# Pooled and banded attention with a gated feed-forward layer on one core: a written step order for the fill and the first eight slots, and seven products for half of the first w_out block

## The chip, the cores and the metric

The kernel runs on one core of one Trainium2 chip. The metric is the device time of one execution in microseconds (us), lower is better. Before the change the median of 5 runs was 346.57 us (345.24 to 352.35).

The core's engines work side by side, each through its own list of instructions in order: PE (matrix products, with PEld loading weights), DVE (vector), ACT (activations), POOL (general), and SP, which here only issues transfers. They meet at semaphores. PE writes its products to eight banks (`ps`), from which DVE and ACT read them.

## The reference

For 8 batches and 8 heads of 576 positions and 64 columns, the attention is the sum of two parts: one over sequences pooled four to one, repeated back, and one over a band of positions less than 4 apart. Its output, seen as 4608 tokens by 512, goes through a gated layer with 1536 inner columns.

```python
q_d = q.reshape(B, H, Sd, 4, D).mean(axis=3)      # k_d, v_d likewise
out_up = np.repeat(sm_attn(q_d, k_d, v_d), 4, axis=2)
mask = np.abs(pos[:, None] - pos[None, :]) < 4
out_local = softmax(np.where(mask, scale * q @ k.T, -1e9)) @ v
x = (out_up + out_local).transpose(0, 2, 1, 3).reshape(4608, 512)
out = (np.maximum(x @ w_gate, 0) * (x @ w_val)) @ w_out
```

## The kernel before

**Units of work.** Heads are taken two at a time: 32 pairs, four to a batch. Tokens of the gated layer are taken in 9 chunks of 512. The attention runs ahead of the layer, by four pairs at first (`LEAD`), because a chunk needs `xT`, the attention's output, of four pairs. So the program has a fill (pairs 0 to 3, with no layer yet), slots 0 to 7 (one pair each, chunks 0 and 1 beside them), steady periods (`emit_periods`, four pairs and one chunk each) and a tail. Each period follows the written order `ORDER`, the tail follows `TAIL`: tokens name a step, and each engine gets the steps' instructions in that order. Fill and slots were written as nested function calls (`emit_fill`, `emit_slot`, `LEAD_IN`).

**A pair.** q, k and v are loaded by POOL's transfers as 16-bit values (`qk`, `vw`; q of pair 0 by SP as 32-bit values, then cast on ACT). For pairs 0 to 8, PE flips q and k in 24 small products of 120 columns (L328): 96 columns are the transposed block, 24 the pooled sums. DVE and ACT copy them out (L348, L350). From pair 9 on a transposing transfer of SP does it (L302) and DVE pools (L309). Then come the scores, pooled (L389) and banded (L400); their exponentials on ACT (L410, L424); the mask on DVE (L416); the pooled v, which pairs 0 to 8 get from PE (L373) with a copy on ACT (L380), and the others from POOL in two additions (L355, L361) of v loaded a second time (L297). The output is made in one of three ways:
- pairs 0 to 3: output products with positions as rows (L447 pooled, L456 banded), reciprocals and multiplications on DVE (L464 to L474) into `xo`, which PE turns back to `xT` (L601, L605) and DVE or ACT copies (L614 to L617);
- pairs 4 to 8: softmax sums (L486, L495) and outputs (L505, L514) as separate half-array products, the sums' logarithm and exponential on ACT (L523, L525), one multiplication on DVE (L528) and one addition into `xT` (L538);
- from pair 9: outputs and sums in one whole-array product (L552, L560), with ACT and DVE working on 64 partitions at a time (L570, L575, L579).

**A chunk.** For each of 12 blocks of inner columns, four products with w_gate and four with w_val (L622), 128 by 512 each; relu on ACT (L639) and the product of the two on DVE (L643) into `gT`. The products with w_out: chunk 0 by 4 blocks of 12 products of 512 columns (L652), one in each of slots 4 to 7, copied out by ACT and stored by ACT's queue. From chunk 1 on, a `Unit` for each half chunk does it with seven products of 6 steps of 256 columns (L718), as in Strassen's scheme, for which DVE forms sums of `gT` (L712) and joins results (L755 to L767), ACT keeps partial results (L752), and DVE once forms four differences of w_out (L685, `emit_wt`).

**Fillers.** Products of zeros (`emit_warm`, L825) stand in the fill, where PE would have nothing to do: ten at the start, 19 of 512 columns afterwards.

**Loads in the fill.** POOL issues q, k and v of pairs 0 to 3, the first slice (of four) of w_gate and w_val, pairs 4 and 5, slice 1, pair 6, slice 2, pair 7, slice 3, q, k and v of pair 8, and four slices of w_out (L262, L292, L794, L800). A slice serves three of the twelve blocks.

Of the kernel before, what the change touches and what calls it, by code (L numbers as in the profile page):

```python
# [17 lines left out]
LEAD_IN = """  # L18
hg/3 relu/3 o/b00 o/b01 o/b10 o/b11 ln/b0 ln/b1 hv/3 gate/3 inv/b hg/4 relu/4 hv/4 xn/b0 gate/4
hg/5 relu/5 hv/5 xn/b1 xsum/b  # L20
# [35 lines left out]
LATE = ("gate/5/1", "next/0/1", "next/1/1")  # L56
# [61 lines left out]
def kernel(  # L118
# [26 lines left out]
    NVP = 9  # L145
# [10 lines left out]
    ffn = ctx.enter_context(tc.tile_pool(name="ffn", bufs=3))  # L156
# [38 lines left out]
    q32 = q32full[0:96]  # L195
    gT = ring(2, [128, NJJ, TCH], FP16, "gT_")
# [3 lines left out]
    wt4 = [xT[:, 0:3, 0:TCH].rearrange("p k (h d) -> p k h d", h=2)]  # L200
    wt4 += [t.rearrange("p (k h) d -> p k h d", h=2) for t in wtnew]
# [42 lines left out]
    def emit_load_qk(hp):  # L244
        for i in range(4):
            emit_load_q1(hp, i)

    def emit_load_q1(hp, i):

        b, off = head_off(hp)  # L250
        src, dst, hh = (q, k)[i // 2], qk16[hp % NL][:, i // 2, :], i % 2
        if hp < NTP:
            if hh:
                return
            if hp == 0 and src is q:
                nc.sync.dma_start(
                    q32.rearrange("p (n d) -> p n d", d=64),
                    _dap(src, off, [[D, 96], [NQ * D, 2 * NB], [1, D]]),
                )
                nc.scalar.copy(out=dst, in_=q32)  # L260
            else:
                nc.gpsimd.dma_start(  # L262
                    dst.rearrange("p (n d) -> p n d", d=64),
                    _dap(src, off, [[D, 96], [NQ * D, 2 * NB], [1, D]]),
                )
            return
        nc.gpsimd.dma_start(  # L267
            dst.rearrange("p (j h d) -> p j h d", h=2, d=64)[:, :, hh, :],
            _dap(src, off + hh * S * D, [[D, 96], [NQ * D, NB], [1, D]]),
        )  # L270
# [45 lines left out]
    def emit_qkT_pe(hp, b0, b1, b0_last=False):  # L316
        r, r4, r2 = hp % NL, hp % 4, hp % 2
        sv = qk16[r].rearrange("p i (h j d) -> p i h j d", h=2, d=64)
        blocks = list(range(2 * NB))
        if hp == 0:  # L320
            blocks = blocks[NB:] + blocks[:NB]
        elif b0_last:
            blocks = blocks[4:] + blocks[:4]
        for n in blocks:
            lo = 120 * (n % 4)
            bank = b0 if n < 4 else b1 + n // 4 - 1
# [8 lines left out]
        big = qkT[r4][:, 0 : 2 * S].rearrange("p (b n t) -> p b n t", b=3, n=4)  # L335
        sml = qkd[r2].rearrange("p i t -> p (i t)").rearrange("p (b n t) -> p b n t", b=3, n=4)
        act, dve = nc.scalar.copy, nc.vector.tensor_copy
        if hp == 0:
            plan = ((2, 1, act), (2, 0, act), (1, 1, dve), (1, 0, dve), (0, 1, act), (0, 0, dve))
        elif b0_last:  # L340
            plan = ((1, 1, act), (1, 0, act), (2, 1, dve), (2, 0, dve), (0, 1, dve), (0, 0, act))
        else:
            plan = ((0, 1, act), (0, 0, act), (1, 1, dve), (2, 1, dve), (2, 0, dve), (1, 0, act))
        for i, pooled, copy in plan:
            bank = b0 if i == 0 else b1 + i - 1
            t = ps[:, bank, 0:480].rearrange("p (n t) -> p n t", n=4)
            if pooled:
                copy(out=sml[:, i], in_=t[:, :, 96:120])  # L348
            else:
                copy(out=big[:, i], in_=t[:, :, 0:96])  # L350
# [16 lines left out]

    def emit_vd(hp, bank):
        t = vw[hp % NL][:, :, 0:64].rearrange("p (h j) d -> p j h d", h=2)
        o = ps[:, bank, 0:256].rearrange("p (c h d) -> p c h d", c=2, h=2)  # L370
        for c in range(2):
            for sig in range(3):
                nc.tensor.matmul(  # L373
                    out=o[:, c, :, :],
                    lhsT=pool_sb[0:WK, sig, :],
                    rhs=t[:, 3 * c + sig, :, :],
                    start=(sig == 0),
                    stop=(sig == 2),
                )
        nc.scalar.copy(  # L380
            out=vd[hp % 3].rearrange("p c (x d) -> p c x d", x=3)[:, :, 0:3:2, :], in_=o[0:72]
# [49 lines left out]
    def emit_s1(hp, p0):  # L431
        emit_s1_mm(hp, p0)
        for g in range(2):
            emit_exp(hp, p0, g)
            emit_mask(hp, g)
        emit_ed(hp, p0)

    def emit_s2(hp, bank, pu):
        r2 = hp % 2
        x = xo[hp % 3]  # L440
        vflat = vw[hp % NL].rearrange("p b c -> p (b c)")
        for hh in range(2):
            for tcx in range(2):
                for c in range(2):
# [4 lines left out]
                        lhsT=ed[r2][:, hh, s0 : s0 + 128],  # L449
# [3 lines left out]
                    )  # L453
        for hh in range(2):
            for j in range(NB):
                nc.tensor.matmul(  # L456
                    out=ps[:, 2 * pu + hh, 65 * j : 65 * j + 65],
                    lhsT=ee[r2][:, hh, NQ * j : NQ * j + 128],
# [4 lines left out]
        rd = small.tile([72, 2, 2], FP32, name="rd", tag="rd")  # L463
        nc.vector.reciprocal(out=rd, in_=_sap(ps, (0, 72), 512 * bank + 64, [[66, 2], [65, 2]]))  # L464
        nc.vector.tensor_tensor(
            out=x[0:72, NB : NB + 2, :].rearrange("p t (h d) -> p h t d", h=2),
            in0=_sap(ps, (0, 72), 512 * bank, [[131, 2], [65, 2], [1, 64]]),
            in1=_sap(rd, (0, 72), 0, [[2, 2], [1, 2], [0, 64]]),
            op=ALU.mult,
        )  # L470
        ru = small.tile([96, 2, NB], FP32, name="ru", tag="ru")
        nc.vector.reciprocal(out=ru, in_=_sap(ps, (0, 96), 1024 * pu + 64, [[448, 2], [65, NB]]))
        for j0, j1 in ((0, 3), (3, 6)) if hp == LEAD - 1 else ((0, 6),):
            nc.vector.tensor_tensor(  # L474
                out=x[:, j0:j1, :].rearrange("p j (h d) -> p h j d", h=2),
                in0=_sap(ps, (0, 96), 1024 * pu + 65 * j0, [[513, 2], [65, j1 - j0], [1, 64]]),
                in1=_sap(ru, (0, 96), j0, [[NB, 2], [1, j1 - j0], [0, 64]]),
                op=ALU.mult,
            )

    def emit_s2t_mm(hp, den, num):
        r2 = hp % 2
        e, d = ee[r2], ed[r2]
        for g in range(2):
            for hh in range(2):
                nc.tensor.matmul(  # L486
                    out=ps[64 * hh : 64 * hh + 64, den + g, 0:288],
                    lhsT=ones_sb[0:WK, 0:64],
                    rhs=e[:, hh, 288 * g : 288 * g + 288],
# [3 lines left out]
            for c in range(2):  # L493
                for hh in range(2):
                    nc.tensor.matmul(  # L495
                        out=ps[64 * hh : 64 * hh + 64, den + g, 288:360],
                        lhsT=ones_sb[0:72, 64:128],
                        rhs=d[:, hh, c * SD + 72 * g : c * SD + 72 * g + 72],
                        start=(c == 0),
                        stop=(c == 1),  # L500
                    )
        for g in range(2):
            for j in range(3):
                for hh in range(2):
                    nc.tensor.matmul(  # L505
                        out=ps[64 * hh : 64 * hh + 64, num + g, NQ * j : NQ * j + NQ],
                        lhsT=vw[hp % NL][:, NB * hh + 3 * g + j, 0:64],
                        rhs=e[:, hh, 288 * g + NQ * j : 288 * g + NQ * j + NQ],
                        start=True,
                        stop=True,  # L510
                    )
            for c in range(2):
                for hh in range(2):
                    nc.tensor.matmul(  # L514
                        out=ps[64 * hh : 64 * hh + 64, num + g, 288:360],
                        lhsT=vd[hp % 3][:, c, 128 * hh : 128 * hh + 64],
                        rhs=d[:, hh, c * SD + 72 * g : c * SD + 72 * g + 72],
                        start=(c == 0),
                        stop=(c == 1),
                    )  # L520

    def emit_rden(den, between=lambda: None):
        nc.scalar.activation(out=rden, in_=ps[:, den : den + 2, 0:360], func=AF.Ln)  # L523
        between()
        nc.scalar.activation(out=rden, in_=rden, func=AF.Exp, scale=-1.0)  # L525
# [3 lines left out]

    def emit_s2t(hp, between):  # L530
        emit_s2t_mm(hp, 4, 2)
        emit_rden(4, between)
        emit_xn(2)
        emit_xsum(hp)
# [51 lines left out]
    def emit_s2w(hp):  # L586
        for hh in range(2):
            for g in range(2):
                emit_s2w_mm(hp, hh, g)
        for hh in range(2):  # L590
            emit_ln(hh)
        emit_inv()
        for hh in range(2):
            emit_xnw(hh)

    def emit_x_pe(hp, pp):
        b, kk = hp // NPB, hp % NPB
        x = xo[hp % 3]
        for g in range(2):
            flat = pair(pp)[:, g, 0:288]  # L600
# [595 lines left out]
```

## Time and profile before

| | us |
|---|---|
| Median of 5 runs (range) | 346.57 (345.24 to 352.35) |
| The profiled execution | 345.24 |
| Its span, first instruction to last | 343.3 |
| PE busy in the span | 336.0 |
| DVE, ACT, POOL busy | 289.9, 215.3, 189.8 |
| First product of chunk 0 with weights (L622) starts | 24.82 |
| First w_out product of the steady periods (L718) starts | 95.07 |

The profile is of one execution. Times of places count from the start of the span. A line such as "17.11 0.60 PE L825 MATMUL ps<-zero_sb 128*128 128x512 f16 x2" gives start, busy time, engine, line of the kernel, operation, what it writes and reads, array rows by columns, and how many instructions were merged; brackets at its end give idle time of the engine before it and what ended it. A matrix product shown as busy overlaps the next, so PE's pace is read from start to start.

### The profile page before, as it was taken

The numbers are of one execution on the slowest core, as the hardware profiler recorded it, in microseconds if no ns is written. First come the engines' busy times: TensorE is split into PE (matmuls) and PEld (weight loads), VectorE is DVE, ScalarE is ACT, GpSimd is POOL, SyncE is SP. The second block draws the span as 40 slices with busy tenths as digits, with TensorE's granted clock in tenths as the row PEclk, the third lists the DMA queues.
The fourth block names the chain that finished last, engine by engine and source line by source line (L and its number), as shares of the span: only waits on it lengthen the run. The fifth ranks groups of instructions, "written<-read, shape, count | busy, mean of one in ns | idle before, by whom it ended". The sixth has DMA issues, their size and how long they took to land.

```text
span 343.3 us, 8159 instructions
## 1 busy us (share of the span) xinstructions
PE 336.0 (98%) x3187; PEld 210.4 (61%) x3187; DVE 289.9 (84%) x529; ACT 215.3 (63%) x410; POOL 189.8 (55%) x233
## 2 busy tenths in 40 slices
PE   6999999999999999999999999999999999999996
PEld 2665555555565756565666656665766557767785
DVE  5895667788899999999999999999999798886892
ACT  3767776677666776677667767776677633334222
POOL 8986656999999894988298879840300000000000
PEclk9999999999999999999999999999999999999999
DMA  9999999999999999999999997991100001001023
GB/s 152 166 170 186 187 189 169 165 152 184 186 155 174 163 170 93 136 157 148 114 113 158 153 126 82 174 133 37 51 13 32 32 0 48 31 33 60 30 65 110
DMA packets 168774, 40.31 MB, mean 117 GB/s; under 512 B 150080, under 2 KB 165664, under 8 KB 168736
## 3 DMA queue, kind: packets, MB, share of 16 engines
q0 software_dynamic: 132960, 22.93, 90.6%
q1 hardware_dynamic: 35056, 15.79, 23.4%
q10 hardware_dynamic: 720, 1.08, 1.0%
q8 instruction: 25, 0.41, 0.5%
q14 instruction: 13, 0.11, 0.1%
HBM read 46.45 MB, written 9.44 MB: 163 GB/s over the span
## 4 chain that ended last, share of the span: by engine, by line
PE 92%; DVE 3%; DMA 2%; ACT 1%; issue 1%; ACTq 0%; POOLq 0%
PE ps L622 50%; PE ps L718 20%; PE ps L928 4%; PE ps L552 3%; PE ps L652 3%; PE ps L400 2%; PE ps L389 2%; PE ps L328 2%; PE ps L560 2%; DMA qk<-in_k_dram 1%; DVE xo L474 1%; PE ps L486 1%; PE ps L373 0%; DMA out_dram<-y_sb 0%; PE ps L601 0%
## 5 line engine op out<-in xcount | busy, mean ns | idle before, releaser
L622 PE MATMUL ps<-xT,wv_sb 128*128 128x512 f16 x432 | 109.3, 379 | 0.0
L622 PE MATMUL ps<-xT,wg_sb 128*128 128x512 f16 x352 | 89.1, 380 | 0.1
L643 DVE TENSOR_TENSOR gT<-r,ps 128x512 f16<-128x512 f16 x88 | 59.2, 681 | 12.0 <-ACT r L639 6.3
L639 ACT ACTIVATE r<-ps 128x512 f16<-128x512 f32 x88 | 52.3, 595 | 26.6 <-PE ps L622 26.4
L622 PEld LDWEIGHTS <-wv_sb 128*128 128x128 f16 x432 | 41.0, 98 | 41.6
L622 PEld LDWEIGHTS <-wg_sb 128*128 128x128 f16 x352 | 32.0, 98 | 32.3 <-DVE xT L615 0.6
L579 DVE TENSOR_TENSOR xn<-ps,rden 64x720 f16<-64x720 f32 x46 | 41.7, 906 | 6.3 <-ACT rden L575 5.2
L410 ACT ACTIVATE ee<-ps 112x576 f16<-112x576 f32 x64 | 38.1, 648 | 10.4 <-PE ps L400 9.3
L570 ACT ACTIVATE rden<-ps 64x720 f32<-64x720 f32 x46 | 35.2, 765 | 14.7 <-PE ps L560 13.7
L267 POOL DMA_DIRECT2D qk<-in_q_dram x46 | 33.7, 735 | 5.1 <-DMA wo_sb<-in_moe_w_out_dram 2.8
L361 POOL TENSOR_TENSOR vd<-v 72x256 f16<-72x256 f32 x23 | 20.0, 877 | 29.8 <-PE ps L560 29.2
L416 DVE TENSOR_TENSOR ee<-ee,cst_sb 112x576 f16<-112x576 f16 x64 | 32.1, 521 | 3.2 <-ACT ee L410 2.2
L267 POOL DMA_DIRECT2D qk<-in_k_dram x46 | 33.7, 735 | 2.0 <-DMA qkT<-qk 1.2
L718 PEld LDWEIGHTS <-gT 128*128 128x128 f16 x288 | 28.2, 98 | 8.6
L292 POOL DMA_DIRECT2D vw<-in_v_dram x30 | 28.5, 949 | 7.7 <-PE ps L622 3.3
L309 DVE TENSOR_REDUCE qkd<-qkT 128x288 f16<-128x1152 f16 x23 | 30.9, 1344 | 0.4 <-DMA qkT<-qk 0.4
L355 POOL TENSOR_TENSOR v<-v 72x512 f32<-72x512 f16 x23 | 28.4, 1233 | 1.8 <-DMA v<-in_v_dram 1.2
L718 PEld LDWEIGHTS <-xo 128*128 128x128 f16 x240 | 22.8, 98 | 6.0 <-DVE xo L712 0.3
L752 ACT COPY q<-ps 128x256 f32<-128x256 f32 x39 | 14.5, 372 | 18.4 <-PE ps L718 17.6
L718 PE MATMUL ps<-wo_sb,gT 128*128 128x256 f16 x192 | 24.9, 273 | 0.0
L938 ACT COPY vw<-ps 128x256 f32<-128x256 f32 x30 | 10.8, 374 | 20.7 <-PE ps L928 13.8
L538 DVE TENSOR_TENSOR xT<-xn 128x576 f16<-128x576 f16 x28 | 21.9, 783 | 0.6
(115 smaller groups left out, 569.6 us busy)
## 6 DMA issues: line engine op xcount, KB each, us to landing
out_dram<-y_sb SPq DMA_DIRECT2D x20, 256.0 KB, 3.2
vw<-in_v_dram POOLq DMA_DIRECT2D x30, 168.0 KB, 6.6
qk<-in_q_dram POOLq DMA_DIRECT2D x46, 72.0 KB, 6.0
qk<-in_k_dram POOLq DMA_DIRECT2D x46, 72.0 KB, 5.8
v<-in_v_dram POOLq DMA_DIRECT2D x23, 144.0 KB, 6.4
out_dram<-y_sb SPq DMA_DIRECT2D x22, 128.0 KB, 1.7
wg_sb<-in_moe_w_gate_dram POOLq DMA_DIRECT2D x4, 384.0 KB, 9.6
wv_sb<-in_moe_w_val_dram POOLq DMA_DIRECT2D x4, 384.0 KB, 10.6
```

Of the source, the lines that this page charges most:

```text
L267: nc.gpsimd.dma_start(dst.rearrange("p (j h d) -> p j h d", h=2, d=64)[:, :, hh, :], _dap(src, off + hh * S * D, [[D, 96], [NQ * D, NB], [ ...
L292: nc.gpsimd.dma_start(t, _dap(v, base, [[D, WK], [NQ * D, n], [1, D]]))
L309: nc.vector.tensor_reduce(out=qkd[hp % 2].rearrange("p i t -> p (i t)"), in_=qkT[hp % 4][:, 0 : 2 * S].rearrange("p (t f) -> p t f", f=4), ...
L355: nc.gpsimd.tensor_tensor(out=m, in0=t[:, :, 0:128], in1=t[:, :, 128:256], op=ALU.add)
L410: nc.scalar.activation(out=o, in_=ps[0:WK, p0 + 2 * g : p0 + 2 * g + 2, 0:288], func=AF.Exp, scale=scale)
L416: nc.vector.tensor_tensor(out=o, in0=o, in1=_sap(masks_sb, (0, WK), 288 * g, [[0, 2], [1, 288]]), op=ALU.mult,)
L570: nc.scalar.activation(out=rden[lo : lo + 64], in_=ps[de : de + 64, 4 + 2 * hh : 6 + 2 * hh, 0:360], func=AF.Ln)
L579: nc.vector.tensor_tensor(out=xn[lo : lo + 64], in0=ps[lo : lo + 64, 4 + 2 * hh : 6 + 2 * hh, 0:360], in1=rden[lo : lo + 64], op=ALU.mult,)
L622: nc.tensor.matmul(out=pair(pp)[:, which, :] if out is None else out, lhsT=w[:, kk, bass.ts(jj, 128)], rhs=xT[:, kk, c * TCH : (c + 1) * TCH],
L639: nc.scalar.activation(out=r1, in_=pair(pp)[:, 0, :] if h1 is None else h1, func=AF.Relu)
L643: nc.vector.tensor_tensor(out=gT[c % 2][:, jj, :], in0=r1, in1=pair(pp)[:, 1, :] if h2 is None else h2, op=ALU.mult)
L718: nc.tensor.matmul(out=out, lhsT=left[:, i, :], rhs=right[i], start=(first and i == 0), stop=(i == NK - 1), skip_group_check=True,)
```

## The change

- Fill and slots 0 to 7 are no longer function calls but one written list, `FRONT`, whose tokens name a step, its pair or block and often the bank and the engine that copies. Every former function that issued several steps is split: a flip into three groups of eight products (`tr/pair/group/bank`) with copies placed by themselves (`ev`), sums and outputs of a pair into halves (`den`, `num`), output products into pooled and banded (`sd`, `su`), a turn back into halves (`xp`, `xe`), pooled v and its copy (`vd`, `vc`), a w_out block into quarters (`y`). Tokens with `@` are steps of the periods' kind.
- Chunk 0: half 0 (two blocks) keeps the plain w_out products, half 1 is done by a `Unit` (`p/..@1`, `sum`, `keep`, `c11` to `c22`). The plain results are stored by SP's queue, not ACT's.
- `NVP` goes from 9 to 11: pairs 9 and 10 get their pooled v from PE too, and their second load of v and POOL's additions go. Pair 8 changes from separate sums to the joint form.
- Fillers: 12 of 512 columns at the start, then 31 of 248 columns.
- v of pair 8 is loaded after w_out's slices and q and k of pair 9. The order of the loads ahead of that stays.
- The first layer products of chunk 0 stand before pair 3's output, and for single depth steps (`hv/0/0/7`: block 0, depth 0, bank 7).
- Relu results lie in a fixed ring of three, the places of w_out's differences are exchanged, and one more gate of chunk 1 is issued with the first steady period (`LATE`).

```diff
+FRONT = """
+pads loadk/0 loadv/0 loadq/1 loadk/1 loadv/1 loadq/2 cast loadk/2 tr/0/2/4 tr/0/1/3 ev/0/21V/4
+loadv/2 tr/0/0/2 ev/0/20V/4 ev/0/10A/3 vd/0/6 ev/0/01A/2 ev/0/00A/2 loadq/3 ev/0/11A/3 vc/0/6
+warm/6 tr/1/0/7 loadk/3 s1/0/2 ev/1/00A/7 tr/1/1/0 ev/1/01A/7 loadv/3 ed/0/2 tr/1/2/1 ev/1/20V/1
+ev/1/11A/0 warm/2 sd/0/6 ex/0/0/2 wg/0 ev/1/21V/1 rd/0/6 td/0/6 ev/1/10A/0 wv/0 ma/0/0 ex/0/1/2
+warm/7 s1/1/0 ones/4 vd/1/6 ma/0/1 ex/1/1/0 su/0/4 loadq/4 ed/1/0 ru/0/4 tu/0/1/4 ex/1/0/0
+warm/4 tr/2/1/2 loadk/4 tu/0/0/4 tr/2/2/3 ev/2/10A/2 tr/2/0/0 ev/2/21V/3 xp/0/1/5 ev/2/20V/3
+loadv/4 ev/2/11A/2 xp/0/0/4 ev/2/00A/0 ma/1/0 ev/2/01A/0 vc/1/6 ma/1/1 warm/3 s1/2/0 ones/5
+xe/0/0A/4 xe/0/1V/5 sd/1/6 ed/2/0 loadq/5 su/1/4 rd/1/6 td/1/6 ex/2/1/0 ru/1/4 warm/3 vd/2/6
+loadk/5 tu/1/1/4 ex/2/0/0 tr/3/1/2 tu/1/0/4 tr/3/2/3 loadv/5 vc/2/6 tr/3/0/0 ev/3/20V/3
+ev/3/10A/2 xp/1/0/4 xp/1/1/5 ma/2/1 ev/3/00A/0 sd/2/6 ev/3/21V/3 xe/1/1V/5 ev/3/11A/2 ev/3/01A/0
+wg/1 ma/2/0 xe/1/0A/4 warm/3 s1/3/0 rd/2/6 td/2/6 su/2/4 ed/3/0 vd/3/6 ru/2/4 tu/2/1/4 ex/3/0/0
+warm/3 hv/0/0/7 tu/2/0/4 wv/1 hv/0/1/7 ex/3/1/0 hv/1/0/1 ma/3/0 xp/2/1/5 vc/3/6 xp/2/0/4 ones/6
+ma/3/1 tr/4/0/0 xe/2/0A/4 xe/2/1V/5 sd/3/6 ev/4/00A/0 hv/1/1/1 loadq/6 rd/3/6 su/3/4 td/3/6
+ev/4/01A/0 hv/0/2/7 ru/3/4 hg/1/0/0 loadk/6 tu/3/1/4 tr/4/1/2 hv/1/2/1 ev/4/10A/2 tu/3/0/4
+tr/4/2/3 loadv/6 hg/0/0/6 ev/4/11A/2 ev/4/20V/3 xp/3/1/5 xp/3/0/4 ev/4/21V/3 hg/1/1/0 xe/3/1V/5
+wg/2 xe/3/0A/4 hg/1/2/0 hg/1/3/0 s1/4/2 wv/2 relu/1/0 hv/1/3/1 ex/4/0/2 hv/0/3/7 gate/1/1
...
+flip/9 num/7/1/7 tr/8/0/0 ev/8/21V/3 inv qk/a3/1@0 ev/8/20V/3 hv/11/*/1 ev/8/01V/0 ev/8/11V/2
+v/a/1@0 ev/8/00A/0 xn/6 y/1/0/3 y/1/1/3 qk/b0/1@0 gate/11/1 scores/a/0@1 xsum/7 qk/b1/1@0 vd/8/1
+exp/a0/0@1 y/0/0/2 qk/b2/1@0 vc/8/1 mask/a0/0@1 y/0/1/2 exp/a1/0@1 sum/0/1@1 qk/b3/1@0 hg/0/0@1
...
+sum/3/1@1 ln/b0/0@1 o/b11/0@1 vd/10/0 sum/2/1@1 p/1/1@1 ln/b1/0@1 pool/a/0@1 v2/b/0@1 hv/2/0@1
...
 """
-LATE = ("gate/5/1", "next/0/1", "next/1/1")
+LATE = ("gate/5/1", "gate/4/1", "next/0/1", "next/1/1")
-    NVP = 9
+    NVP = 11
-    def emit_qkT_pe(hp, b0, b1, b0_last=False):
...
+    def emit_flip(hp, i, bank):
+
+        sv = qk16[hp % NL].rearrange("p i (h j d) -> p i h j d", h=2, d=64)
+        for n in range(4 * i, 4 * i + 4):
             lo = 120 * (n % 4)
...
+    def emit_flipped(hp, i, pooled, eng, bank):
...
+        copy_on(eng)(out=o[:, i], in_=t[:, :, 96:120] if pooled else t[:, :, 0:96])
-    def emit_y(c, ty, bank, cut=0, inner=None):
...
+    def emit_y(c, ty, q, bank):
+        for jj in range(3 * q, 3 * q + 3):
             nc.tensor.matmul(
-                out=y_ps,
+                out=ps[:, bank, :],
                 lhsT=gT[c % 2][:, jj, bass.ts(ty, 128)],
                 rhs=wo_sb[:, jj, :],
                 start=(jj == 0),
                 stop=(jj == NJJ - 1),
             )
...
-        emit_out(c, ty, y_sb, nc.scalar)
+        emit_out(c, ty, y_sb, nc.sync)
...
+    def emit_front(tok):
+        kind, *a = tok.split("/")
+        if "@" in tok:
+            emit_step(kind, a[0], *map(int, a[1].split("@")))
         else:
+            FRONT_STEPS[kind](*[int(x) if x.isdigit() else x for x in a])
...
-        emit_warm(10)
-        emit_qkT_pe(0, 2, 3)
-        emit_pads()
-        emit_warm(3)
-        for hp in range(LEAD):
-            emit_fill(hp)
-        gate = None
-        for s in range(PS):
-            gate = emit_slot(s, gate)
+        emit_warm(12, True)
+        for tok in FRONT.split():
+            emit_front(tok)
         emit_periods(PS // 4, (NP - LEAD) // 4)
```

## The prediction

> **What bounds the kernel now.** The page first: which engine has no air, and whether the clock is granted.
>
> ```profile
> PE 336.0 (98%) x3187; PEld 210.4 (61%) x3187; DVE 289.9 (84%) x529; ACT 215.3 (63%) x410; POOL 189.8 (55%) x233
> ...
> PE   6999999999999999999999999999999999999996
> PEclk9999999999999999999999999999999999999999
> DMA  9999999999999999999999997991100001001023
> ...
> PE 92%; DVE 3%; DMA 2%; ACT 1%; issue 1%; ACTq 0%; POOLq 0%
> ```
>
> PE is busy from slice 2 to the end at full granted clock, and the chain that ended last is PE for 92%. But a filler product counts as busy too, so the question is what PE's first stretch holds. Next the same view by stretches: the fill, chunk 0, the rest of what the change rewrites, and one steady period.
>
> ```profile
> 6.31:24.82 18.51, 16.87 (x331) 12.22 (x331) 16.15 (x49) 12.08 (x30) 17.27 (x22) 1.00 2.20 166
> 24.82:57.60 32.78, 32.66 (x420) 18.18 (x416) 21.07 (x44) 24.86 (x50) 19.15 (x25) 1.00 1.73 185
> 57.60:95.07 37.47, 37.47 (x312) 18.95 (x307) 29.79 (x40) 25.98 (x42) 35.86 (x44) 1.00 1.88 170
> ...
> 130.86:166.00 35.14, 35.14 (x324) 21.93 (x323) 33.73 (x52) 24.92 (x45) 26.80 (x33) 1.00 1.65 140
> ```
>
> Columns: stretch, length, PE, PEld, DVE, ACT, POOL busy with counts, granted clock, DMA, GB/s. From 24.82 on PE is full; only the fill has idle time. The order of time in the fill says what else is in it:
>
> ```profile
> 17.11 0.60 PE L825 MATMUL ps<-zero_sb 128*128 128x512 f16 x2
> ...
> 17.91 0.28 PE L601 MATMUL ps<-cst_sb,xo 72*128 72x288 f16 x1 [0.20 <-DVE xo L474]
> ...
> 18.50 0.82 PE L328 MATMUL ps<-cst_sb,qk 96*64 96x120 f16 x24
> ...
> 24.82 0.82 PE L622 MATMUL ps<-xT,wv_sb 128*128 128x512 f16 x3
> ```
>
> Two fillers (L825) hold PE from 17.11 to 17.91 until DVE has written xo; the next pair is flipped (L328) at 18.50, 3.97 us after the last one. The first useful product of the chunk (L622) starts at 24.82. Last, when its weights were there:
>
> ```profile
> 12.00 0.77 POOL L794 DMA_DIRECT2D wv_sb<-in_moe_w_val_dram  x1
> ...
> 21.34 0.75 POOL L794 DMA_DIRECT2D wv_sb<-in_moe_w_val_dram  x1 [1.08 <-DMA wv_sb<-in_moe_w_val_dram]
> ```
>
> The first slice of w_val, issued at 12.00, lands 9.05 us later, at 21.05 (the view of that one transfer gives 9.0 to landing). So 3.7 us pass between the weights' arrival and their first use. That is the air; after it, everything up to the first steady step (L718, 95.07) is PE end to end.
>
> **The change, part by part.** I set PE's end of the rewritten stretch, 95.07, against what it becomes.
>
> *When the first weight product can start.* The written order puts it behind the flips, scores and pooled v of four pairs, the output products of three and the turning back of two. POOL issues its first 33 transfers, up to k of pair 8, in the same order as before, so 21.05 stays. Does PE reach it by then? I laid the new lists side by side with rows of the fill, start to start: eight flip products 0.20 (24 take 0.75 with the switch), scores 0.40, pooled v 0.33, the eight products of the pooled output 0.25, the twelve of the local one 0.37, fillers 0.103 (248 of 512 columns at 0.213). On ACT a 384-column copy holds the engine 0.37, a 96-column one 0.14, an exponential 0.54, the pooled exponential 0.53; on DVE copies 0.46 and 0.17, masks 0.40 each, the normalizing steps 0.20, 0.34, 0.25 and twice 0.47, the copy to xT 0.38. Results pass 0.06 us after their end to PE, 0.2 from PE to ACT or DVE. Scores then start at 8.5, 11.0, 14.6 and 18.7 (before: 8.42, 12.29, 16.21, 20.19); pair 3's pooled v waits for DVE's step on pair 2 and starts at 20.0; three fillers end at 20.6. PE then waits 0.5 for w_val: start **21.1**. Behind that new wait stands all of PE's list; ACT and DVE still have pair 3's exponentials and masks to do, so they lose nothing. If passing results is 0.1 slower at each of the eight hand-overs between 11 and 20, the start is 21.9: the ends are 21.1 and 21.9, and I take 21.1, because the sum came out below the landing.
>
> *What is left for PE from there.* Before: 95.07 - 24.82 = 70.25. Changes:
> - Now behind that point: pair 4's flip 0.60, pair 3's two output products 0.62, pair 2's turn 0.50: +1.72.
> - w_out: four blocks of 12 products of 512 columns become two, 24 x 0.216 = 5.19 less, and 7 x 6 products of 256 columns come, 42 x 0.109 = 4.59 (L718 in the steady periods: 12 in 1.31): -0.60. The 18 further weight loads (98 ns) run beside the products there already.
> - Pooled v of pairs 9 and 10 by PE instead of POOL: two times 0.33 (L373, 12.80 to 13.14): +0.67; ACT gets two copies of 0.37 beside 25.98 busy of 37.47. POOL loses two loads and four additions, 2 x (0.73 + 1.17 + 0.73) = 5.3 us; PE waits for none of them, so nothing.
> - Pair 8's output with the sums in the same product: 0.79 for 0.81: nothing.
> - Switches between whole-array and half-array products (flip, scores, sums with a 64-column weight). Here is what one costs:
>
> ```profile
> 33.95 1.04 PE L622 MATMUL ps<-xT,wg_sb 128*128 128x512 f16 x4
> 34.82 1.03 PE L622 MATMUL ps<-xT,wv_sb 128*128 128x512 f16 x4
> 35.78 0.25 PE L389 MATMUL ps<-qkd 64*72 64x144 f16 x2
> ...
> 38.11 0.82 PE L328 MATMUL ps<-cst_sb,qk 96*64 96x120 f16 x24
> 38.87 1.04 PE L622 MATMUL ps<-xT,wg_sb 128*128 128x512 f16 x4
> ```
>
> Four products take 0.87 before another four (33.95 to 34.82), but 0.96 ahead of half-array ones: 0.10 to go in; the 24 flips take 0.76 for 0.60 of columns: 0.10 to 0.15 to come out. The new order cuts flips in three and sums in two. Counted along both lists behind the first weight product: 17 such visits before, 20 after: 3 x 0.22 = +0.66. Five times a flip or sum stands directly beside scores, one half-array form beside another: no row has that, so 0 to 0.10 each; I take the middle, +0.25.
> - Before's wait for xT inside the first group (26.21 to 27.15 for three products, 0.30) goes.
> Sum: 70.25 + 1.72 - 0.60 + 0.67 + 0.66 + 0.25 - 0.30 = 72.65; 21.1 + 72.65 = **93.75** with no new wait.
>
> The Trainium skill, TensorEngine Tiling (Array Packing), "Key Properties", says that changing the tiling mode drains the engine, and names no price. It speaks against cutting flips and sums into pieces. Where rows have it they agree (0.10 in, 0.12 out); on the five neighbours of two half-array forms it would ask the full price, 72.9 in place of 72.65, and a row alone would let them go free, 72.4.
>
> *New waits.* Groups now stand closer to their evictions. Carried on from 21.1, the lists give four: 0.2 on xT of pair 3 in the fourth gate product, 0.1 on a gate before pair 5's pooled v, 0.2 on gate 3 before pair 6's flip, 0.4 on the flip's copies before pair 6's pooled v; 0.9 up to 37 us. Each hangs on my 0.2 hand-over; at 0.1 they are 0.3. Ends: 0 and, if the next 57 us are no better than the first 16, 2.4. Nearest is the old order, which has nearly none after 27 us. I take **0.4**. Arrivals have little air too: w_gate slice 1 lands at 28.99 and is asked for at 29.5, k of pair 7 at 39.73 for 40.2, others 0.4 to 5 us; v of pair 8, now behind three w_out slices, pair 9's q and k and the fourth slice, lands near 57.2 (46.60 + 4 x 1.9 + 1.95 + 1.05) and is asked for at 59. These margins cost nothing, but they cap what a faster PE could gain near 0.5.
>
> *DVE, ACT, SP.* Between 57.6 and 95 DVE had 29.8. It gets the four sums 2.5, three joins 1.25, pair 8 in halves 0.9: 34.4 to 34.8. ACT gets three keeps of 0.37 and a copy of 0.36 for two of 0.59, and one more logarithm, 0.77: 1.1 beside 26.0. That fits only as the steady period does (33.73 in 35.14). SP takes the w_out rows that ACT issued (0.35 each); they stand behind flips that wait for q and k, and only the four-deep y ring waits for them: nothing. The transposes move up with q and k of pair 9, by about 3 us: nothing.
>
> *The first steady period* took 35.94 (95.07 to 131.01), the next 35.46. Of the 0.48, 0.35 is one wait (99.55) for DVE's sums. DVE comes fuller to it now: 0 to -0.35, or +0.5 if it is late; I take 0.
>
> Total: 93.75 + 0.4 - 95.07 = **-0.9**. The profiled execution took 345.24 (span 343.3), the lowest of five and 1.3 under the median; -0.9 makes it 344.3, and the median 346.57 - 0.9 = **345.7**.
>
> The fillers also keep PE's clock: the first ten take 0.425 each, later ones 0.213. The gap of 0.53 ahead of the flips at 10.61 cost the products behind it nothing, and the longest that I find in the new lists is 0.5, so narrower fillers are free.
>
> **Rivals.**
> 1. *No new waits, and the first period loses its 0.35.* 21.1 + (72.65 - 0.25) = 93.5, so -1.57 - 0.35 = -1.9: 344.7. For it: the old order waits almost nowhere after 27. Against: two groups stand directly behind the copies that free their bank.
> 2. *The fill is no faster.* ACT and DVE set its pace, 3.2 and 3.6 us a pair by the sums above, and PE comes at 21.9, with waits of 0.5 behind it: 21.9 + 72.65 + 0.5 = 95.05: 346.6. For it: DVE is at 16.15 of 18.51 there already; against: scores at 18.7 leave 2 us.
> 3. *DVE becomes the bound of chunk 1, and it is slower.* Its 34.4 after the last gate of chunk 0 (57.9 by my lists) reach 92.3; DVE sat idle 7.7 in that stretch before, 2.6 of it on ACT's relu. With 5.5 idle it ends at 97.8, +2.7: 349.3. It decides from 2.8 idle on, and the kernel is slower by 0.5% from 4.5. Against: steady periods wait under 1.8.
>
> **How the numbers follow.** Forecast 0.42, rivals 0.25, 0.17 and 0.16. 0.5% is 1.7 us, about what a measurement of this kernel can tell from no change. Rival 1 is faster, and 0.07 of the forecast through its lower end: 0.32; the rest of the forecast and rival 2 same: 0.52; rival 3 slower: 0.16. The forecast's own range is 344.8 to 346.5. For 8 in 10: down to rival 1 less 1.1, a part of the 1.85 between the three middle runs, 343.6; up to where half of rival 3 is in, 348.7.
>
> **What will show it.** The first L622-kind product at 21.1, after a short wait on w_val; scores of pair 3 near 18.7; the first steady w_out product near 94.2; pieces of flips costing 0.3 each; DVE above 34 between 57.6 and there. Wrong if that first product starts after 22, if waits between 30 and 57 sum to over 1.5, or if DVE ends PE's waits after 60.

## The result, and the profile after

| | before | after |
|---|---|---|
| Median, us (before 93 runs, after 51) | 347.67 (345.24 to 352.35) | 349.35 (346.80 to 353.19) |
| Ratio, 95% interval | | 1.0044 [1.0032, 1.0056] |
| Profiled execution (span) | 345.24 (343.3) | 349.53 (347.7) |
| First w_val slice lands | 21.05 | 21.64 |
| First weight product of chunk 0 | 24.82 | 23.99 |
| First steady w_out product | 95.07 | 97.97 |
| From there to the last product's end | 245.02 | 246.48 |

The changed kernel is 1.7 us slower. That is inside the 0.5% taken as about what can be told from no change, but the interval lies above 1. The forecast was 0.9 us faster, and the measured time lies 0.65 us above the range. Of the 3.65 us between the forecast, 345.7, and 349.35, 1.1 is the base: the forecast started from a median of 5 runs, 346.57, where 93 runs give 347.67. Ratios here and below leave out executions that took over 1.5% more than the fastest of their kernel.

The page of the changed kernel, its busy times, three rows of the 40 slices and its chain:

```profile
PE 338.0 (97%) x3219; PEld 214.2 (62%) x3219; DVE 294.0 (85%) x537; ACT 218.4 (63%) x421; POOL 185.4 (53%) x227
...
PE   6899999999999999999999999999999999999996
PEclk9999999999999999999999999999999999999999
DMA  9999999999999999999979996992000001001023
...
PE 92%; DVE 3%; DMA 2%; ACT 2%; issue 1%; DVEq 0%; ACTq 0%; POOLq 0%
```

PE still ends the chain, at the same 92%, and no other engine has taken its place. The stretches show more: the fill, chunk 0, and chunk 1 with the seven products, of the changed kernel (columns: stretch, length, PE, PEld, DVE, ACT, POOL busy with counts, clock, DMA, GB/s).

```profile
6.50:23.99 17.49, 14.50 (x291) 11.60 (x292) 10.43 (x30) 12.26 (x33) 15.81 (x20) 1.00 2.18 167
23.99:60.05 36.06, 35.60 (x468) 19.87 (x466) 24.11 (x51) 26.43 (x54) 23.26 (x30) 1.00 1.78 180
60.05:97.97 37.92, 37.88 (x328) 21.55 (x327) 32.74 (x49) 27.12 (x47) 31.99 (x41) 1.00 2.13 162
```

From 60 on PE is full, so DVE has not become the bound there. In the fill PE is idle for 3.0 of 17.5 us, 0.54 of it until k of pair 0 has landed at 6.99; the prediction had gaps of at most 0.5 and a wait of 0.5 for w_val. What PE waits for stands in the order of time of the fill, PE alone:

```profile
9.14 0.80 PE L810 MATMUL ps<-zero_sb 128*128 128x248 f16 x6 [0.69 <-ACT vd L416]
...
12.74 0.90 PE L810 MATMUL ps<-zero_sb 128*128 128x248 f16 x7 [0.80 <-DVE xo L503]
...
17.33 0.48 PE L810 MATMUL ps<-zero_sb 128*128 128x248 f16 x3 [0.34 <-ACT vd L416]
...
19.46 0.48 PE L810 MATMUL ps<-zero_sb 128*128 128x248 f16 x3 [0.42 <-DVE xo L503]
...
23.99 0.81 PE L638 MATMUL ps<-xT,wv_sb 128*128 128x512 f16 x3
```

Behind the first flips (7.04), every wait of more than 0.15 us is that of a filler (L810), a product of zeros that nobody needs. The narrow fillers write columns 264 to 511 of bank 6. The pooled v and the pooled output products of the fill go to columns below 264 of the same bank, and each filler behind them waits until ACT has copied them (`vd`, L416) or DVE has used them (`xo`, L503). The four waits add up to 2.25 us, and the first weight product starts 2.35 us after its weights have landed. Before the change the fillers stood in bank 7, which nothing else in the fill used. So the change moved them as well as narrowing them:

```diff
-                out=ps[:, 7, :], lhsT=zero_sb[:, 0:128], rhs=zero_sb[:, 128:640], start=True, stop=True
+                out=ps[:, 7, :] if wide else ps[:, 6, 264:512],
...
+                rhs=zero_sb[:, 128 : 640 if wide else 376],
```

The profile finds what ended a wait from semaphores, by which this program orders its engines. The waits therefore show that the program makes a filler wait for readers of other columns of its bank; whether the chip itself would need that, no run tried.

### The profile page after: what moved, and what is told of

It is laid out like the page before. It is cut to its first block, busy times and chain, and to the rows that moved or that the text cites. A ratio compares the mean times of both kernels' runs of the same rounds, so it can differ in the third digit from the quotient of the medians.

```text
span 347.7 us, 8209 instructions
## 1 busy us (share of the span) xinstructions
PE 338.0 (97%) x3219; PEld 214.2 (62%) x3219; DVE 294.0 (85%) x537; ACT 218.4 (63%) x421; POOL 185.4 (53%) x227
## 4 chain that ended last, share of the span: by engine, by line
PE 92%; DVE 3%; DMA 2%; ACT 2%; issue 1%; DVEq 0%; ACTq 0%; POOLq 0%
PE ps L638 49%; PE ps L722 21%; PE ps L903 4%; PE ps L584 4%; PE ps L437 2%; PE ps L426 2%; PE ps L592 2%; PE ps L363 2%; DMA qk<-in_k_dram 2%; PE ps L654 1%; PE ps L407 1%; PE ps L810 1%; DVE xo L716 1%; DVE qkT L377 0%; PE ps L527 0%
## 5 line engine op out<-in xcount | busy, mean ns | idle before, releaser
L611 DVE TENSOR_TENSOR xn<-ps,rden 64x720 f16<-64x720 f32 x48 | 43.5, 905 | 4.2 <-ACT rden L607 2.6
L602 ACT ACTIVATE rden<-ps 64x720 f32<-64x720 f32 x48 | 36.7, 765 | 15.4 <-PE ps L592 14.4
L722 PEld LDWEIGHTS <-gT 128*128 128x128 f16 x306 | 29.9, 98 | 9.2
L391 POOL TENSOR_TENSOR vd<-v 72x256 f16<-72x256 f32 x21 | 17.9, 859 | 28.8 <-PE ps L592 28.5
L722 PEld LDWEIGHTS <-xo 128*128 128x128 f16 x264 | 25.1, 97 | 7.9 <-issue 0.7
L385 POOL TENSOR_TENSOR v<-v 72x512 f32<-72x512 f16 x21 | 27.3, 1302 | 3.8 <-DMA v<-in_v_dram 3.3
L756 ACT COPY q<-ps 128x256 f32<-128x256 f32 x42 | 15.6, 372 | 20.5 <-PE ps L722 20.2
L722 PE MATMUL ps<-wo_sb,gT 128*128 128x256 f16 x204 | 26.5, 273 | 0.0
L722 PE MATMUL ps<-wt,xo 128*128 128x256 f16 x198 | 25.4, 272 | 0.2 <-DVE xo L716 0.2
L570 DVE TENSOR_TENSOR xT<-xn 128x576 f16<-128x576 f16 x28 | 23.6, 844 | 0.4
```

What stands on the lines that cost most here:

```text
L385: nc.gpsimd.tensor_tensor(out=m, in0=t[:, :, 0:128], in1=t[:, :, 128:256], op=ALU.add)
L602: nc.scalar.activation(out=rden[lo : lo + 64], in_=ps[de : de + 64, 4 + 2 * hh : 6 + 2 * hh, 0:360], func=AF.Ln)
L611: nc.vector.tensor_tensor(out=xn[lo : lo + 64], in0=ps[lo : lo + 64, 4 + 2 * hh : 6 + 2 * hh, 0:360], in1=rden[lo : lo + 64], op=ALU.mult,)
L722: nc.tensor.matmul(out=out, lhsT=left[:, i, :], rhs=right[i], start=(first and i == 0), stop=(i == NK - 1), skip_group_check=True,)
```

## The experiments

Three theories stood against each other. **Theory 1**: the narrow fillers' bank makes PE wait, and this is the whole loss. **Theory 2**, the prediction's second rival: ACT and DVE set the fill's pace, and the fillers only show a wait that the next real product would have had. **Theory 3**: the stretch behind the first weight product (up to the first steady w_out product) costs more than was summed, by changes between whole-array and half-array products, by new waits, or by the work that was traded. Where an edit below begins with "bank 7", its kernel is the changed one with the fillers in bank 7, the third of the runs.

**Both kernels once more.** No edit.

> The kernel before, unchanged, for a second profile on the same chip as the next three. It tells what of the 4.4 us between the two profiled spans is the change and what is a quick execution: the first profile was of the lowest of all runs. If the change is what shows, the first weight product starts at 24.8 again and the first steady w_out product at 95.1 within 0.3, and the span after that is 248.2 again. If the first profile was a quick execution, the first k lands near 7.0 and not 6.26, all of the fill is some 0.7 later (weight product near 25.5), and the steady part takes 1 to 2 us more than 248.2.

> The changed kernel, unchanged, as the base for its variants on this chip. Ratio to before 1.004, first weight product near 24.0, first steady w_out product near 98.0, both within 0.5.

Measured: before 349.14 in the one execution that was profiled; after 349.38, 1.0048 [1.0019, 1.0076] against 347.45, the median of 29 further executions of the kernel before on that chip. The first profile of before was a quick execution: in the second, k of pair 0 lands at 7.36, the first weight product starts at 26.50, the first steady w_out product at 97.14, and what follows takes 250.1 in place of 248.2. In the changed kernel's second profile the two marks are 25.08 and 98.85, both off by more than the 0.5 expected. In both profiled executions the granted clock fell to half for 3.41 us, from 8.7 to 12.1 and from 8.8 to 12.2; the fill's row of the second (same columns as above):

```profile
6.50:24.00 17.50, 14.84 (x274) 11.71 (x275) 9.39 (x28) 11.31 (x31) 16.62 (x21) 0.90 2.18 166
```

One such stretch brings the mean granted clock of an execution to 0.995. It was 0.995 or less in 28 of the 93 executions of the kernel before that were taken beside the variants, and in 8 of 64 of the changed kernel. Both orders have such executions, so this does not explain why the changed one is slower; it widens the scatter of both. The difference between the kernels itself repeats.

**The narrow fillers in bank 7.** The changed kernel with one number changed:

```diff
-                out=ps[:, 7, :] if wide else ps[:, 6, 264:512],
+                out=ps[:, 7, :] if wide else ps[:, 7, 264:512],
```

> The changed kernel with its 31 narrow fillers written to columns 264 to 511 of bank 7 in place of bank 6, where the pooled products and their readers are. Nothing else changes. Theory 1 (fillers wait): in the profile of the changed kernel the fillers at 9.14, 12.74, 17.33 and 19.46 start after waits of 0.69, 0.80, 0.34 and 0.42 that end with ACT's copy or DVE's step that reads bank 6, and PE's list stands behind them; in bank 7 nobody reads, so most of these 2.25 us go, the first weight product starts at 21.7 to 22.3 (the w_val slice landed at 21.64), and the time falls by 1.5 to 2.3 us to a ratio of 0.998 to 1.000 against before. Theory 2 (ACT and DVE set the fill's pace): the waits only move to the next score or turn; first weight product after 23.5, time within 0.5 us of the changed kernel. Theory 3 (the loss lies behind the first weight product): the start moves, but the first steady w_out product does not.

Measured: 347.39, 1.0000 [0.9974, 1.0026], against 349.38 of the changed kernel on the same chip: 2.0 us back. The order of time in its fill, PE alone:

```profile
7.72 0.80 PE L810 MATMUL ps<-zero_sb 128*128 128x248 f16 x6
...
10.36 0.90 PE L810 MATMUL ps<-zero_sb 128*128 128x248 f16 x7
...
14.55 0.48 PE L810 MATMUL ps<-zero_sb 128*128 128x248 f16 x3
...
16.09 0.48 PE L810 MATMUL ps<-zero_sb 128*128 128x248 f16 x3
...
20.57 0.48 PE L810 MATMUL ps<-zero_sb 128*128 128x248 f16 x3
20.89 0.81 PE L638 MATMUL ps<-xT,wv_sb 128*128 128x512 f16 x3
```

The same groups of fillers as above, with no wait ahead of any. Bank 7 is not wholly their own in the new order, as the expectation has it: one group of pair 1's flips (`tr/1/0/7`) goes there and ACT copies it, but that copy was done before the next fillers came. The weights landed at 20.56 here and are used at 20.89. Theory 2 falls: ACT and DVE keep up, and the products behind the fillers wait at most 0.3 in the fillers' place (pooled v of pair 2, 16.67 for 16.40). The scores of pairs 0 to 3 start at 8.78, 11.20, 14.96 and 19.06, and the first w_out product of the steady periods at 94.65, for 97.97. Theory 3 asked that this mark stay, so it does not explain the loss; that the stretch in front of it is longer than was summed is taken up under the prediction.

**No narrow fillers.** The changed kernel with the 31 left out:

```diff
+        "warm": lambda n: None,
```

> The changed kernel without its 31 narrow fillers (they compute nothing that is used). Theory 1: as with bank 7, the waits go, and the 3.2 us of fillers as well where nothing else is late; first weight product at 21.7 to 22.3, time 1.5 to 2.3 us under the changed kernel, if the clock holds. If PE's clock falls without fillers, products of the fill take about twice as long in the profile (eight flips 0.4 and not 0.2) and the start comes after 25. Theory 2: start after 23.5 again.

Measured: 347.91, 1.0006 [0.9975, 1.0037]; first weight product at 20.79, weights at 20.74, clock 1.00 in the fill of its profile. It can't be told from bank 7, so fillers that wait for nothing cost nothing that shows. In this one profile their work for the clock was not needed, but in other executions its lack shows: three of the 12 have a mean granted clock of 0.979 to 0.980 (348.85, 350.43 and 351.38 us), and the ratio leaves the two longest out. With the fillers in bank 7 none of 12 is below 0.998.

**The old order with narrow fillers, in bank 7 and in bank 6.** A test in the other direction: the kernel before, where the 16 fillers between the fill's steps become 248 columns wide, in one case in bank 7, in the other in bank 6 (the lines shown; the calls inside the fill pass `wide` as false).

```diff
-                out=ps[:, 7, :], lhsT=zero_sb[:, 0:128], rhs=zero_sb[:, 128:640], start=True, stop=True
+                out=ps[:, 7, :] if wide else ps[:, 6, 264:512],
+                lhsT=zero_sb[:, 0:128],
+                rhs=zero_sb[:, 128 : 640 if wide else 376],
```

> The kernel before with the 16 fillers that stand inside its fill narrowed from 512 to 248 columns, still in bank 7: the control for the next run. PE's fill there waits for DVE and ACT, so less filler changes the start of the first weight product by less than 0.7 us earlier, and the time by less than 0.7.

> The same, with these 16 fillers in columns 264 to 511 of bank 6, where pooled products lie in columns 0 to 259. Theory 1: the fillers behind the pooled v wait for ACT's copy of it, which ACT does after the exponentials (14.33 to 14.70 in the old profile, while the fillers stood at 13.14), and PE's list waits with them: 0.8 to 1.5 us a pair, first weight product 2.5 to 5 us later than in the control, and the time 2 to 5 us more. If a bank's other columns don't matter: no difference to the control.

Measured: bank 7 347.31, 1.0008 [0.9977, 1.0039]; bank 6 359.71, 1.0354 [1.0308, 1.0400]. The bank was expected to cost 2 to 5 us and cost 12.4. The fill of the bank-6 kernel, PE alone in order of time:

```profile
11.02 0.48 PE L825 MATMUL ps<-zero_sb 128*128 128x248 f16 x3 [1.43 <-ACT vd L380]
...
13.63 0.37 PE L825 MATMUL ps<-zero_sb 128*128 128x248 f16 x1 [0.66 <-DVE xo L465]
...
16.57 0.57 PE L825 MATMUL ps<-zero_sb 128*128 128x248 f16 x2 [0.95 <-ACT vd L380]
...
18.03 1.41 PE L328 MATMUL ps<-cst_sb,qk 96*64 96x120 f16 x24
19.37 0.62 PE L447 MATMUL ps<-vd,ed 72*128 72x65 f16 x8
...
23.74 0.57 PE L825 MATMUL ps<-zero_sb 128*128 128x248 f16 x2 [0.96 <-ACT vd L380]
```

and its stretches 6.5 to 24 and 24 to 60 (columns as above):

```profile
6.50:24.00 17.50, 12.82 (x196) 9.67 (x193) 10.89 (x34) 8.84 (x21) 16.76 (x21) 0.70 2.18 166
24.00:60.00 36.00, 34.65 (x415) 21.36 (x414) 21.75 (x47) 20.93 (x44) 22.04 (x29) 0.81 1.77 182
```

The same waits as in the changed kernel, longer: 4.0 us in the four shown, and 0.96 in a fifth at 30.91. The second part was not expected: from 13.64 the granted clock stays at half for 23.89 us. The 24 flips take 1.34 (18.03 to 19.37) in place of 0.75. The first weight product starts at 35.94; in the bank-7 kernel it starts at 25.08, with the clock at 1.00. All six executions in bank 6 have a mean granted clock between 0.953 and 0.965, and none of the 12 in bank 7 is below 0.994. So the bank works in both orders, and its price has two terms: the waits, and the clock where PE is idle too often. In the changed kernel the fillers wait less, and its first profile shows the first term alone. How the 12.4 us divide between the two, no run shows.

**Sixteen wide fillers at the start.** Bank 7, and more work for PE before k of pair 0 lands:

```diff
-        emit_warm(12, True)
+        emit_warm(16, True)
```

> Fillers in bank 7 as in the run before, and 16 wide fillers at the start in place of 12. In two profiled executions, one of the old kernel and one of the changed one, the granted clock was 0.5 for one window of 3.41 us at 8.7 to 12.2, after PE had waited more than a microsecond for the first k; the others show no such window. Theory 4 (the early clock): fillers that reach to the landing of k (12 end near 6.4, 16 end near 7.0) take that window away; median 0.4 to 1.0 us under the kernel with 12, and no clock of 0.5 after 6 us. If the window is not what sets the median, within 0.3 us of the kernel with 12; the first weight product waits for w_val either way and starts within 0.3 us of its landing.

Measured: 346.94, 0.9983 [0.9953, 1.0013]. Not to be told from 1. Theory 4 finds no support: none of the 12 executions has a mean granted clock below 0.999, but with 12 wide fillers in bank 7 none was below 0.998 either, so there was no half-clock stretch left to take away. The first weight product starts at 22.10, after a wait of 0.64 for w_val, which lands at 22.06.

**Half 1 of chunk 0 by plain products.** Bank 7, with two plain w_out blocks (`y/2`, `y/3`) in place of the seven-product unit:

```diff
-y/0/3/2 ... sum/2/1@1 p/1/1@1 ... keep/1/1@1 ... c11//1@1 ... c12//1@1
+y/0/3/2 ... y/2/0/0 ... y/3/3/1 ... yout/3/1
```

> Fillers in bank 7; the second half of chunk 0 by two plain blocks of 12 products of 512 columns again, so the four sums, three joins and three kept copies of that half go; pooled v of pair 10 a little earlier, since its bank is then in use. From the first weight product to the first steady w_out product the kernel with the seven products took 73.76. By the prediction's term the seven products are 0.60 cheaper on PE: 74.4 here. If DVE was what held PE in that part (rival 3), the 4.3 us of DVE work that go are worth more than 0.60: under 73.5.

Measured: 348.35, 1.0002 [0.9975, 1.0029]. In its profile the stretch behind the start is 1.51 longer than in the bank-7 kernel: 0.58 of it is products and 0.93 waits, 0.87 of them one wait of PE for a mask on DVE, of a kind that is told at the end. At 75.27 it is not under 73.5, so the work that went was not what held PE. The ratio is no worse than bank 7's, so the trade of 0.6 us of products is too small to see in the time of the kernel.

**Pooled v of pairs 9 and 10 back on POOL.** Bank 7, with

```diff
-    NVP = 11
+    NVP = 9
```

and POOL's additions (`v4`, `v2`, `v1`) back in the list.

> Fillers in bank 7; pooled v of pairs 9 and 10 by POOL from a second load of v again, 12 products fewer on PE. By the prediction's term 0.67 less between the two marks: 73.1. If POOL or the transfers hold something up after that, the same or more than 73.8.

Measured: 346.58, 0.9961 [0.9938, 0.9983], the lowest ratio of all. The stretch behind the start is 73.25 against 73.76; 0.69 of products went, and 0.18 of waits came. The ratio's interval still overlaps that of bank 7.

**Fewer visits to half-array products.** Bank 7, with three whole-array groups moved past a piece of a flip, of sums and of outputs:

```diff
-tr/4/1/2 hv/1/2/1 ... den/5/1/5 relu/6/0 tr/6/0/4 hv/5/*/7 ... num/6/0/2 gate/7/3 hg/9/*/0
+hv/1/2/1 tr/4/1/2 ... hv/5/*/7 den/5/1/5 relu/6/0 tr/6/0/4 ... hg/9/*/0 num/6/0/2 gate/7/3
```

> Fillers in bank 7; three weight products (block 1 depth 2 of w_val, block 5 of w_val, block 9 of w_gate) are moved ahead of half-array products that they stood between, so PE changes form three visits fewer. By the price of 0.10 in and 0.12 out from the old trace: 0.66 less between the two marks, 73.1, if no new wait comes. If cutting is free and only waits count: 73.6 to 73.9.

Measured: 347.09, 0.9985 [0.9958, 1.0013]. The first move gave 0.27 (first weight product to pair 4's scores, 5.50 for 5.77). The second met a wait that was not there before; the order of time, PE alone:

```profile
39.62 0.38 PE L311 MATMUL ps<-cst_sb,qk 96*64 96x120 f16 x8
40.85 0.31 PE L475 MATMUL ps<-ee,ones_sb 112*64 112x288 f16 x2 [0.86 <-ACT qkT L325]
```

The sums of pair 5 (L475) now stand directly behind the flip whose copy frees their bank, without the four products of w_val between. So the moves saved six changes, 0.58, and lost 1.03 here (from start to start, as counted under the prediction; the 0.86 in brackets counts from the end of the busy time). The whole stretch takes 74.36, where 73.1 was expected if no wait came.

**Pooled v of pair 6 later.** Bank 7, with `vd/6/1` moved behind `hg/5/*/6`, to let the flip's copy in bank 1 end:

```diff
-vd/6/1 ma/5/1 ev/6/10A/0 hg/5/*/6 xn/2 ex/5/0/4 loadk/8 hg/6/*/0
+ma/5/1 ev/6/10A/0 hg/5/*/6 xn/2 ex/5/0/4 loadk/8 vd/6/1 hg/6/*/0
```

> The changed kernel with fillers in bank 7 and one PE step moved: the pooled v of pair 6 behind block 5 of w_gate in place of ahead of it. In that place PE lost 0.61 to DVE's copies of the flip, the largest wait between the first weight product and 60 us. If such waits are the missing part of the sum: scores of pairs 4 to 8 lie 31.7 to 31.9 apart and not 32.32. If the wait passes on to the next step that needs ACT or DVE: 32.2 or more.

Measured: 346.60, 0.9976 [0.9948, 1.0005]. The wait did not go, it moved. The order of time of the bank-7 kernel and of this one, PE alone:

```profile
35.33 0.41 PE L363 MATMUL ps<-cst_sb,qk 96*64 96x120 f16 x8
36.14 0.50 PE L407 MATMUL ps<-vw,cst_sb 112*128 112x128 f16 x6 [0.40 <-DVE qkd L377]
```

```profile
35.57 0.40 PE L311 MATMUL ps<-cst_sb,qk 96*64 96x120 f16 x8
36.47 1.02 PE L586 MATMUL ps<-xT,wg_sb 128*128 128x512 f16 x4 [0.50 <-ACT ed L409]
```

Pooled v in bank 1 waited for DVE's copy; the gate products in its place wait for ACT's pooled exponential (`ed`, L409), which reads their bank and stands behind another exponential. From pair 4's scores to pair 8's it is 32.42 for 32.31, and the stretch takes 75.08, with a wait of 1.05 for a mask on DVE (shown at the end). The lower median is not explained by this edit.

**A version from these.** Bank 7, `NVP = 9`, sixteen wide fillers and the first of the three moves.

> What paid, together: fillers in bank 7, 16 wide ones at the start, pooled v of pairs 9 and 10 by POOL, and one visit fewer (block 1 depth 2 of w_val ahead of two flip groups). From the first weight product to the first steady w_out product 73.76 - 0.51 - 0.27 = 73.0; median 1.3 to 2.3 us under the kernel before (ratio 0.9935 to 0.9965). If the parts don't add up, 0.997 or more.

Measured: 347.04, 0.9970 [0.9944, 0.9997]. Its one profiled execution took 1215.49 us and is not read, so the expected 73.0 stays without a measurement. It beats the kernel before, but no more than `NVP = 9` in bank 7 alone does.

## Why the prediction was wrong

**The step that failed** is the start of the first weight product. The prediction laid the lists side by side, counted "fillers 0.103" with no wait of their own, and closed with "narrower fillers are free". It looked at the filler's width and not at where it writes. The rest of that walk was right within 0.4: in bank 7 the scores start at 8.78, 11.20, 14.96 and 19.06 where it had 8.5, 11.0, 14.6 and 18.7, and PE comes to the first weight product at 20.89, where the walk had 20.6. The slice had landed at 20.56 by then, so there is no wait for w_val; where it landed later, at 21.35 and 22.06 (fewer visits, sixteen wide fillers), PE waited 0.54 and 0.64 for it, as the prediction asks. With bank 6 it is 23.99, by the prediction's own sign ("after 22") wrong. Its bound, 21.9, was for slower hand-overs at every step, and could not hold a wait that was left out; by its own numbers it should have been 21.4, since eight times 0.1 come on top of 20.6 and not of 21.1, where PE is waiting already. The measured time is near the third rival's 349.3 by luck, not by its mechanism.

**The stretch behind the start.** Predicted 72.65 and 0.4 of waits, 73.05; measured 73.76 in the bank-7 kernel. To split it I took each product's start to the next one's start, less its columns (512 in 0.213), put 0.096 to each change between array forms, and called what was left, over 0.03, a wait. The last row but one is a remainder and was not measured by itself.

| term | predicted | measured |
|---|---|---|
| changes of the array form | 0.66 + 0.25 | 45 for 34, 11 x 0.096 = 1.06 |
| waits | 0.4 - 0.30 | 0.98 for 0.56, +0.42 |
| pooled v of pairs 9 and 10 | 0.67 | 0.69 |
| moved steps and seven products | 1.72 - 0.60 | 1.34, as what is left of 3.51 |
| sum over 70.25 | 2.80 | 3.51 |

- *Changes.* The counts were right, 17 visits before and 20 after, and five places where one half-array form stands directly beside another. A visit costs 0.19, not 0.22. For the five neighbours I took 0.05 each, the middle; each costs the full 0.10. In the bank-7 kernel, PE alone in order of time:

```profile
34.68 0.29 PE L437 MATMUL ps<-qkT 64*128 64x96 f16 x6
34.93 0.40 PE L363 MATMUL ps<-cst_sb,qk 96*64 96x120 f16 x8
35.14 0.32 PE L548 MATMUL ps<-ee,vw 112*64 112x96 f16 x6
...
41.07 0.40 PE L363 MATMUL ps<-cst_sb,qk 96*64 96x120 f16 x8
41.40 0.25 PE L426 MATMUL ps<-qkd 64*72 64x144 f16 x2
```

Eight flips take 0.21 ahead of output products of the same form, 64 columns of the array (34.93 to 35.14), and 0.33 ahead of scores, 64 rows of it (41.07 to 41.40). So the trace agrees with the rule that the prediction weighed, the Trainium skill's TensorEngine Tiling (Array Packing), "Key Properties", that a change of mode drains the engine, between two half-array forms as well: the full price is paid there, and 72.9 was the better of the two sums.

- *Waits.* The walk gave four, 0.9 in all, and the trace has 0.98: 0.14 at pair 2's turning back, 0.22 in the fourth gate product, 0.15 before pair 5's pooled v, 0.47 before pair 6's. Three of the places are the ones that it named. The prediction then took 0.4 "nearest the old order"; the order that it was to judge was the one whose lists it had in hand, and its own 0.9 was the better figure. Even that holds for the stretch up to 37 us only. The same list behind the start was profiled five times (the changed kernel twice, bank 7, no narrow fillers, sixteen wide ones) and took 73.76 to 74.87, with 0.98 to 2.08 of waits by the same count; nearly all of the difference is PE waiting for a mask on DVE between 72 and 84. So the bank-7 profile is the best of five, and half a microsecond between single profiles of this stretch proves nothing by itself; the counts of changes and products repeat.
- *Seven products.* 0.60 predicted; the kernel with plain products has 0.58 more in this stretch.

**The rest.** Nothing came of DVE as the bound of chunk 1 (rival 3): PE is busy 37.88 of 37.92 us there, and DVE has 32.74 busy, under the 34 that was to show. In two of the other profiles of this list PE waits 0.73 and 0.95 there, each time for one late mask. The first steady period, scores to scores, takes between 35.6 and 36.8 us in four profiles with the old order and between 35.5 and 37.4 in nine with the new, so the 0 that was taken for it can be neither confirmed nor refuted at 0.35. The profiled execution of before, the base of the sum, was the lowest of 93; the 1.46 that the steady part is longer in the table above is in that scatter, since the kernel before has 246.85 there in its second profile.

**What the sum says.** The forecast's place of the first steady w_out product was 94.15. The bank-7 kernel has it at 94.65, start 0.2 earlier and stretch 0.7 longer, and its time is that of the kernel before. So with the fillers out of bank 6 the change would have been worth about what was forecast less 0.5, which is nothing that can be measured. The bank's 2.0 us made it a loss. The 3.65 us between forecast and measurement are about 1.1 of base, 2.0 of bank and 0.5 of these two marks; that they add up so well is partly luck, since the marks of one kernel lie 0.9 to 2.1 us apart in its two profiles.

## What to carry to other kernels

A product that only fills time still has an output, and its bank has readers: before calling a filler free, list who else writes and reads the bank it goes to, since PE takes its list in order and hands the filler's wait to everything behind it. When lists laid side by side give a sum of waits, take that sum, not a smaller one by likeness to the old order. Count changes of the array form one by one, 0.096 us each here, half-array beside half-array included (two forms of the same 64 columns beside each other cost nothing), and expect that a group moved to save one loses its distance from the copy that frees its bank.

## What was not expected of the hardware

**The clock.** In the second profiles of both kernels the granted clock is halved for one stretch of 3.41 us early in the fill, after PE was idle for 1.85 us (before) and 0.65 us (changed) ahead of the first flips; the old order with bank-6 fillers stays at half for 23.89 us, where its longest wait is 1.43 us. So waits well under 3.41 us can bring it down, while one of 1.46 us in the first profile of the changed kernel and one of 1.73 us in that with `NVP = 9` did not. The runs do not show where the border is.

**Masks beside POOL.** The mask on DVE (`ee` times a constant, two operands in SBUF) takes 0.44 to 0.46 us in every case where POOL does nothing at the time (17 to 24 of the 64 masks in each of 13 profiles). Beside POOL most take that too, but some take up to 2.36 us. In the kernel with the later pooled v, POOL and DVE in order of time, then PE:

```profile
79.55 1.44 POOL L256 DMA_DIRECT2D qk<-in_k_dram  x2
79.77 2.73 DVE L401 TENSOR_TENSOR ee<-ee,cst_sb 112x576 f16<-112x576 f16 x2
81.00 1.16 POOL L333 TENSOR_TENSOR v<-v 72x512 f32<-72x512 f16 x1
...
82.54 0.29 PE L532 MATMUL ps<-ee,vw 112*128 112x96 f16 x3 [1.05 <-DVE ee L401]
```

Two masks end at 82.50, after POOL's addition has ended (82.16), and PE's output products wait 1.05 for them. The Trainium skill, SBUF — State Buffer, "SBUF: two separate sides", says that DVE and GpSimd share one pair of ports by a lock held for a whole instruction, and that a DVE instruction with two operands in SBUF is blocked by a GpSimd instruction that reads SBUF. The addition agrees with it; that a mask is also held beside POOL's issue of a transfer (1.41 us at 88.35 in the kernel before, with nothing but such issues at the time) goes beyond that sentence. In four of the profiles PE's longest wait between 60 and 245 us, 0.71 to 1.05, is one for such a mask, between 72 and 84; in the others no wait for a mask is over 0.5. That they come from the ports was not tried by a run of its own: it is read from the overlap alone.
